# Gated attention with an expert layer on one core: first queries' scores over 128 keys, plain products with v padded to 128 rows, a weight decoding that joins the low and sign bits first, and Newton steps later in a slot

## The chip, the cores and the metric

The kernel runs on one core of one Trainium2 chip. The metric is device time in microseconds of one execution. Three runs of the kernel before took 1253.56, 1248.98 and 1240.35 us, a median of 1248.98. The profiled execution took 1239.64 us, with a span of 1237.4 us from the first to the last instruction.

## The reference

The input is q, k and v of 8 batches x 8 heads x 576 positions x 64, a forget factor f per position, a norm gain g and two weight matrices in float64. Attention with a decay comes first, then a norm and a two-layer network with a residual:

```python
scores = scale * np.matmul(q, k.transpose(0, 1, 3, 2))
log_f = np.log(np.clip(f, 0.0001, 1.0))
cum = np.cumsum(log_f, axis=-1)
decay = cum[:, :, :, None] - cum[:, :, None, :]
scores = np.where(causal, -1000000000.0, scores + decay)
scores = scores - np.max(scores, axis=-1, keepdims=True)
attn = np.exp(scores)
attn = attn / (np.sum(attn, axis=-1, keepdims=True) + 1e-09)
x = np.matmul(attn, v)                      # then heads joined: (8, 576, 512)
xn = (x - mu) / np.sqrt(var + 1e-06) * g_ln
out = x + np.maximum(xn @ w_ch1, 0.0) @ w_ch2
```

w_ch1 is 512 x 2048 and w_ch2 is 2048 x 512. They reach the chip as pairs of 32-bit words, and the kernel itself turns each float64 into a float32, and that into a high part (the type fp32r) and a low part, the rest.

## The kernel before, in words

**Attention.** There are 64 heads. The queries of a head come in five tiles t = 0 to 4 (`QT`): the first 64 queries see 64 keys, and then four tiles of 128 queries see 192, 320, 448 and 576 keys. A slot is one head and one of t = 1 to 4; t = 0 is done together with t = 1, so there are 256 slots. A slot goes: scores on PE (`qk_mm`, L360 or L362 and L363), reduction with mask and minimum on VectorE (`softmax_a`, L386), exponential with a row sum on ScalarE (`softmax_e`, L397), reciprocal of the sum on VectorE (L402, L403), scaling on POOL (`softmax_b`, L404). Two slots later (`LAG`) PE transposes the probabilities (`transpose_unit`, L410) and ScalarE copies them from PSUM to the tiles `ph1` and `ph2` (L460). One slot after that the product with v follows (`av_unit`), once after t = 2 and once after t = 4.

**Two kinds of heads.** The first 16 heads are plain (`h.full`): their products are of float32, and a product appears as two records in the trace. In their product with v (`fac`, L475) 64 rows of the result lie in the lower or upper half of PSUM's partitions, by the query (`SPLIT`), so a tile has 64 columns of weights. The first 64 keys stand alone as k = 0: a product over 64 rows (`rows = slice(0, 64)`), while all others go over 128 rows. The host has sent v with the first 64 rows twice, so all 128 rows of that block of v are filled. The other 48 heads are split into high and low fp32r parts (L362, L363, L500).

**The weights.** While plain heads run, `WPrep` decodes the two matrices in 32 blocks of 128 x 512 numbers, alternately of layer 1 and layer 2. A tick starts a block and carries on the earlier ones: a load from DRAM into `wr` (high and low words alternate), a scaled copy of the high words on ScalarE (`scaled`, L165, into PSUM tile `y`), three steps on VectorE (`decode`), for layer 1 a column sum on PE (L192, `pc`) and four centring steps on VectorE (L200), then the high part on ScalarE (L216) and the low part on POOL (L220). The three decoding steps before are

```python
lambda: ve.tensor_scalar(out=z, in0=z, scalar1=0x80000000, ...),     # L176: sign, in place in wr
lambda: ve.scalar_tensor_tensor(out=y, in0=y, scalar=3, in1=z, ...), # L177: y shifted, sign joined, in PSUM
lambda: ve.scalar_tensor_tensor(out=w, in0=low, scalar=29, in1=y, ...), # L180: low bits joined, into wy
```

`W_SLOTS`, `W_CHANGE` and `W_TICKS` set when ticks are due: one in 2.4 slots up to slot 34, then 0.8 a slot. `wy` has 5 buffers (`W_FLOAT`), `wr` 3. The first 15 blocks (`W_ACC`) use two PSUM tiles that the expert layer needs later; the others take one of the six PSUM banks (`bank`) that scores, transposes, products and hidden values share as well.

**The expert layer.** From slot 35 on (`FIRST_MOE`) a slot also takes one step j of the expert layer for a chunk of 256 tokens, if its weights and inputs are ready: twelve products into `h` (L579 to L581), ScalarE's ReLU (L587), VectorE's low part (L592), and one slot later six products of 512 columns (L601 to L603). A chunk has 16 steps, and there are 18 chunks. The norm's 1/sqrt is worked out on POOL by Newton steps (`chunk_rstd`, L646 to L654) that are kept in a list and run six at a time (`run_later`).

**The order.** It is written out by hand. `ORDERS` holds one string per range of slots, and each letter is a piece: W ticks, w, g and f run 1, 2 and 3 of the queued decoding steps, Q scores, S reduction, e exponential, t transposes, h their copies, A product with v, F and a its finish, M, r, m and N the expert step, R the chunk's upkeep, L the Newton steps, P loads and splits of later heads, B reciprocal and scaling. Each engine works through its instructions in that order. The scaled copy of a block is put at place 5 of the queue of the tick before (`W_ASIDE`) for the first 15 blocks, and for the others it is issued in the tick itself, just ahead of the block's three steps. All DMAs are issued from SP's queue.

Of the kernel before, what the change touches and what calls it, by code (L numbers as in the profile page):

```python
# [8 lines left out]
F32 = mybir.dt.float32  # L9
F32R = mybir.dt.float32r  # L10
U32 = mybir.dt.uint32
# [23 lines left out]
W_ACC = 15  # L35
W_SUMS = 2
# [13 lines left out]
    (37, "WwQSstAMhPelgLNFrfmBRa"),  # L50
    (66, "AthQFlMSPNreamLRB"),
# [4 lines left out]
def attn_moe(ctx: ExitStack, tc: tile.TileContext, qk, v, f, g, w1, w2, out):  # L56
# [79 lines left out]
    class WPrep:  # L136
# [21 lines left out]
        def scaled(self, n):  # L158
            layer, j = self.items[n]
            d = self.d[n]  # L160
            if n < W_ACC:
                d["y"] = ps.tile([P, DM], F32, tag=f"acc{n % 2}", bufs=1, name=f"y{layer}_{j}")
            else:
                d["y"] = bank(f"y{layer}_{j}")
            nc.scalar.activation(d["y"], d["hw"].bitcast(F32), AF.Copy, scale=2.0**-112)  # L165

        def decode(self, n):
            layer, j = self.items[n]
            d = self.d[n]
            y, z, low = d["y"].bitcast(U32), d["hw"], d["lw"]  # L170
            w = wpool.tile([P, DM], U32, tag="wy", bufs=W_FLOAT, name=f"wy{layer}_{j}")
            d["w"] = w.bitcast(F32)
            ve = nc.vector

            return [
                lambda: ve.tensor_scalar(out=z, in0=z, scalar1=0x80000000, scalar2=None, op0=ALU.bitwise_and),  # L176
                lambda: ve.scalar_tensor_tensor(  # L177
                    out=y, in0=y, scalar=3, in1=z, op0=ALU.logical_shift_left, op1=ALU.bitwise_or
                ),
                lambda: ve.scalar_tensor_tensor(  # L180
                    out=w, in0=low, scalar=29, in1=y, op0=ALU.logical_shift_right, op1=ALU.bitwise_or
                ),
            ]
# [39 lines left out]
        def tick(self):  # L223
# [27 lines left out]
            if on(t) and t >= W_ACC:  # L251
                self.scaled(t)
# [6 lines left out]
            if on(t + 1) and t + 1 < W_ACC:  # L259
                self.queue.insert(min(W_ASIDE, len(self.queue)), lambda: self.scaled(t + 1))  # L260
# [90 lines left out]
    def qk_mm(h, t):  # L351
        q0, m, w = QT[t]
        cuts = [(0, w)] if w <= 512 else [(0, w // 2), (w // 2, w)]
        h.s = getattr(h, "s", {})
        h.s[t] = []
        for i, (a, z) in enumerate(cuts):
            sp = bank(f"s{h.n}_{t}_{i}")[:m, : z - a]
            xq, kl = h.xq[:, q0 : q0 + m], h.kl[:, a:z]
            if h.full:
                mm(sp, xq, kl, start=True, stop=True)  # L360
            else:
                mm(sp, h.hi[:, 0, q0 : q0 + m], h.hi[:, 1, a:z], start=True, stop=False)  # L362
                mm(sp, xq, kl, start=False, stop=True)  # L363
            h.s[t].append((a, z, sp))

    corners = []
# [49 lines left out]
    def transpose_unit(h, t):  # L416
# [3 lines left out]
        if t <= 2:  # L420
            if t == 1:
                h.ph1 = work.tile([P, 704], F32 if h.full else F32R, tag="ph1", bufs=1, name=f"ph1_{n}")
                h.pl1 = None if h.full else pools["late"].tile([P, 384], F32R, tag="pl1", bufs=1, name=f"pl1_{n}")
# [15 lines left out]
        else:  # L439
            if t == 3:  # L440
                h.ph2 = work.tile([P, 9 * P], F32 if h.full else F32R, tag="ph2", bufs=1, name=f"ph2_{n}")
                h.pl2 = None if h.full else pools["late"].tile([P, 7 * P], F32R, tag="pl2", bufs=1, name=f"pl2_{n}")
# [24 lines left out]
    def av_unit(h, t):  # L467
        po = bank(f"o{h.n}_{t}")

        if h.full:  # L470

            def fac(cols, k, mv, first=False):
                rows = slice(0, 64) if k == 0 else slice(0, P)
                half = slice(0, 64) if cols.start < SPLIT[t] else slice(64, P)
                mm(po[half, cols], h.vr[rows, k], mv[rows], start=first, stop=True, skip_group_check=True)  # L475
# [415 lines left out]
```

## Time and profile before

| what | value |
|---|---|
| median of three runs | 1248.98 us |
| profiled execution | 1239.64 us |
| its span | 1237.4 us |
| PE busy | 1216.3 us (98%) |
| VectorE busy | 758.5 us (61%) |
| ScalarE busy | 641.8 us (52%) |
| POOL busy | 448.0 us (36%) |
| the chain that ended last, PE's share | 90% |

Instructions are named by engine, line, operation and tiles. PE is a product, PEld a load of weights; products are pipelined and their ends are modelled, so a busy PE may still be waiting inside. In a shape such as `66*64 66x64` the first pair is the rows and columns of the array that are used, and the last number is the columns that stream through. Brackets hold the idle time of the engine ahead of the instruction, and what ended it. The clock is the share of full speed that PE was granted.

### The profile page before, as it was taken

The numbers are of one execution on the slowest core, as the hardware profiler recorded it, in microseconds if no ns is written. First come the engines' busy times: TensorE is split into PE (matmuls) and PEld (weight loads), VectorE is DVE, ScalarE is ACT, GpSimd is POOL, SyncE is SP. The second block draws the span as 40 slices with busy tenths as digits, with TensorE's granted clock in tenths as the row PEclk, the third lists the DMA queues.
The fourth block names the chain that finished last, engine by engine and source line by source line (L and its number), as shares of the span: only waits on it lengthen the run. The fifth ranks groups of instructions, "written<-read, shape, count | busy, mean of one in ns | idle before, by whom it ended". The sixth has DMA issues, their size and how long they took to land.

```text
span 1237.4 us, 25314 instructions
## 1 busy us (share of the span) xinstructions
PE 1216.3 (98%) x8368; PEld 1084.8 (88%) x8368; DVE 758.5 (61%) x2664; ACT 641.8 (52%) x1936; POOL 448.0 (36%) x765
## 2 busy tenths in 40 slices
PE   8998999999999999999999999999999999999998
PEld 6656877899999999999999999999999999999997
DVE  6777673477677767676767676777777662222222
ACT  6886564455555555555655565556555542112111
POOL 3553344344343435444444444444444320000000
PEclk9997998999999999999999999999999999999999
DMA  6554341222323232222222222222222301110100
GB/s 189 151 163 138 112 140 50 70 74 75 94 77 94 77 94 72 88 83 75 71 81 90 81 89 78 76 86 85 71 75 73 94 33 39 52 35 23 46 26 26
DMA packets 91251, 100.44 MB, mean 81 GB/s; under 512 B 26864, under 2 KB 76016, under 8 KB 91120
## 3 DMA queue, kind: packets, MB, share of 16 engines
q1 hardware_dynamic: 91120, 98.82, 26.5%
q8 instruction: 67, 1.10, 0.4%
q14 instruction: 64, 0.52, 0.1%
HBM read 79.61 MB, written 19.17 MB: 80 GB/s over the span
## 4 chain that ended last, share of the span: by engine, by line
PE 90%; DVE 3%; ACT 3%; DMA 1%; issue 1%; POOL 1%; SPq 0%; DVEq 0%; ACTq 0%; POOLq 0%
PE h L579 11%; PE h L580 11%; PE h L581 11%; PE acc L601 11%; PE acc L602 11%; PE acc L603 10%; PE tr L410 7%; PE o L500 6%; PE s L362 3%; PE s L363 3%; PE s L360 2%; PE o L475 2%; PE xp L410 1%; DVE p L386 1%; ACT p L397 1%
## 5 line engine op out<-in xcount | busy, mean ns | idle before, releaser
L404 POOL TENSOR_SCALAR p<-p,st 64x64 f32<-64x64 f32 (+4 forms) x320 | 169.6, 534 | 451.7 <-DVE st L403 156.0
L579 PE MATMUL h<-x,w1h 128*128 128x256 f32 x1152 | 330.1, 287 | 0.5 <-DVE st L386 0.5
L580 PE MATMUL h<-x,w1h 128*128 128x256 f32 x1152 | 326.2, 283 | 0.0
L581 PE MATMUL h<-x,w1l 128*128 128x256 f32 x1152 | 326.2, 283 | 0.0
L587 ACT ACTIVATE hh<-h 128x256 fp32r<-128x256 f32 x288 | 110.6, 384 | 310.4 <-PE h L581 310.3
L592 DVE SCALAR_TENSOR_TENSOR hh<-h,hh 128x256 fp32r<-128x256 f32 x288 | 121.1, 421 | 184.6 <-ACT hh L587 178.0
L601 PE MATMUL acc<-w2h,hh 128*128 128x512 f32 x576 | 228.4, 397 | 0.0
L602 PE MATMUL acc<-w2l,hh 128*128 128x512 f32 x576 | 227.6, 395 | 0.0
L579 PEld LDWEIGHTS h<-x,w1h 128*128 128x128 f32 x1152 | 219.9, 191 | 6.1 <-DVE st L386 0.9
L603 PE MATMUL acc<-w2h,hh 128*128 128x512 f32 x576 | 224.7, 390 | 0.0
L580 PEld LDWEIGHTS h<-x,w1h 128*128 128x128 f32 x1152 | 220.6, 191 | 3.3
L581 PEld LDWEIGHTS h<-x,w1l 128*128 128x128 f32 x1152 | 220.4, 191 | 0.0
L397 ACT ACTIVATE p<-p,st 64x64 f32<-64x64 f32 (+4 forms) x320 | 178.3, 558 | 65.9 <-DVE st L386 64.0
L460 ACT CAST ph<-tr 64x128 fp32r<-64x128 f32 (+4 forms) x384 | 109.1, 333 | 126.2 <-PE tr L410 103.4
L410 PE MATMUL tr<-identr,p 128*128 128x128 f32 (+1 forms) x896 | 142.5, 275 | 5.3 <-POOL p L404 4.7
L386 DVE CUSTOM_DVE_ANT_0 p<-s,mask 64x64 f32<-64x64 f32 (+4 forms) x320 | 130.2, 420 | 5.0 <-PE s L360 1.6
L603 PEld LDWEIGHTS acc<-w2h,hh 128*128 128x128 f32 x576 | 108.3, 188 | 24.9
L410 PEld LDWEIGHTS tr<-identr,p 128*128 128x128 f32 (+1 forms) x896 | 100.9, 131 | 33.3 <-POOL p L404 15.0
L465 DVE TENSOR_TENSOR ph<-tr,ph 64x192 fp32r<-64x192 f32 x192 | 57.8, 301 | 117.1 <-ACT ph L460 114.2
L601 PEld LDWEIGHTS acc<-w2h,hh 128*128 128x128 f32 x576 | 109.5, 190 | 14.1 <-issue 0.3
L602 PEld LDWEIGHTS acc<-w2l,hh 128*128 128x128 f32 x576 | 109.5, 190 | 11.8
L340 POOL TENSOR_TENSOR hi<-raw,hi 64x576 fp32r<-64x576 f32 x48 | 73.8, 1537 | 66.7 <-ACT hi L338 65.3
(83 smaller groups left out, 1846.9 us busy)
## 6 DMA issues: line engine op xcount, KB each, us to landing
raw<-in_qk_dram SPq DMA_DIRECT2D x48, 576.0 KB
wr<-in_w_dram SPq DMA_DIRECT2D x32, 512.0 KB
vr<-in_v_dram SPq DMA_DIRECT2D x64, 160.0 KB
out_dram<-xt SPq DMA_DIRECT2D x36, 256.0 KB
xa<-xs SPq DMA_DIRECT2D x32, 160.0 KB
xb<-xs SPq DMA_DIRECT2D x32, 128.0 KB
xw<-xa SPq DMA_DIRECT2D x64, 64.0 KB
xw<-xb SPq DMA_DIRECT2D x48, 64.0 KB
```

Source lines behind the costliest of these rows:

```text
L386: nc.vector.tensor_tensor_reduce(out=pt[:m, a:z], in0=sp, in1=mask[:m, off + a : off + z], scale=-SCALE, scalar=3.0e38 if i == 0 else st[: ...
L397: nc.scalar.activation(pt[:m, :w], pt[:m, :w], AF.Exp, bias=st[:m, i : i + 1], scale=-1.0, accum_out=st[:m, 2:3])
L404: nc.gpsimd.tensor_scalar(out=pt[:m, :w], in0=pt[:m, :w], scalar1=st[:m, 3:4], scalar2=1.0, op0=ALU.mult, op1=ALU.mult)
L410: nc.tensor.transpose(out_, in_, ident[:m, :m])
L579: mm(ph, w1h[:, k, fs], c.x[k][:, 0, :], start=(k == 0), stop=False)
L580: mm(ph, w1h[:, k, fs], c.x[k][:, 1, :], start=False, stop=False)
L581: mm(ph, w1l[:, k, fs], c.x[k][:, 0, :], start=False, stop=(k == KT - 1))
L587: nc.scalar.activation(h[:, 0, :], c.ph, AF.Relu)
L592: nc.vector.scalar_tensor_tensor(out=h[:, 1, :], in0=ph, scalar=0.0, in1=h[:, 0, :].bitcast(F32), op0=ALU.max, op1=ALU.subtract)
L601: mm(c.acc[i], h[:, 0, ts_], w2h[:, j, :], start=(j == 0), stop=False)
L602: mm(c.acc[i], h[:, 0, ts_], w2l[:, j, :], start=False, stop=False)
L603: mm(c.acc[i], h[:, 1, ts_], w2h[:, j, :], start=False, stop=(j == FT - 1))
```

## The change

Four edits, all in the first quarter of the program's slots but for the one of the Newton steps and the wider key range.

1. *First queries' scores.* Plain heads multiply 128 queries by 128 keys for t = 0, and only 64 x 64 of the result is read. Split heads multiply their 64 queries by 128 keys.
2. *Plain products with v.* `ph1` and `ph2` become two tiles that live for all plain heads, with rows 64 to 127 of the k = 0 part set to zero once by POOL. The k = 0 product then goes over 128 rows like the others.
3. *Decoding.* The scaled copy goes to the SBUF tile `wy` and always stands at place 5 of the queue of the tick before. The three steps are: low words shifted right by 29 into a PSUM tile; sign bits of the high words joined to it there; scaled copy shifted left by 3 and joined with it, in place in `wy`. The high words in `wr` are no longer overwritten.
4. *Newton steps.* The letter L moves behind B in the second and third order.

```diff
+W_BORROW = 2
 ORDERS = [
     (0, "WwQsSthAeMrgFBmlLNPaRf"),
-    (37, "WwQSstAMhPelgLNFrfmBRa"),
-    (66, "AthQFlMSPNreamLRB"),
+    (37, "WwQSstAMhPelgNFrfmBLRa"),
+    (66, "AthQFlMSPNreamRBL"),
 ]
         def scaled(self, n):
-            if n < W_ACC:
-                d["y"] = ps.tile([P, DM], F32, tag=f"acc{n % 2}", bufs=1, name=f"y{layer}_{j}")
+            if layer == 1 and self.tick_no < W_BORROW:
+                d["y"] = m2(f"wy{layer}_{j}", U32)
             else:
-                d["y"] = bank(f"y{layer}_{j}")
-            nc.scalar.activation(d["y"], d["hw"].bitcast(F32), AF.Copy, scale=2.0**-112)
+                d["y"] = wpool.tile([P, DM], U32, tag="wy", bufs=W_FLOAT, name=f"wy{layer}_{j}")
+            nc.scalar.activation(d["y"].bitcast(F32), d["hw"].bitcast(F32), AF.Copy, scale=2.0**-112)
         def decode(self, n):
+            def last():
+                ...   # t: acc tile for n < W_ACC, else a bank
+                ve.tensor_scalar(out=bits[0], in0=low, scalar1=29, scalar2=None, op0=ALU.logical_shift_right)
             return [
-                lambda: ve.tensor_scalar(out=z, in0=z, scalar1=0x80000000, scalar2=None, op0=ALU.bitwise_and),
+                last,
                 lambda: ve.scalar_tensor_tensor(
-                    out=y, in0=y, scalar=3, in1=z, op0=ALU.logical_shift_left, op1=ALU.bitwise_or
+                    out=bits[0], in0=high, scalar=0x80000000, in1=bits[0], op0=ALU.bitwise_and, op1=ALU.bitwise_or
                 ),
                 lambda: ve.scalar_tensor_tensor(
-                    out=w, in0=low, scalar=29, in1=y, op0=ALU.logical_shift_right, op1=ALU.bitwise_or
+                    out=y, in0=y, scalar=3, in1=bits[0], op0=ALU.logical_shift_left, op1=ALU.bitwise_or
                 ),
             ]
         def tick(self):
...
-            if on(t) and t >= W_ACC:
-                self.scaled(t)
...
-            if on(t + 1) and t + 1 < W_ACC:
+            if on(t + 1):
                 self.queue.insert(min(W_ASIDE, len(self.queue)), lambda: self.scaled(t + 1))
     def qk_mm(h, t):
+        if t == 0:
+            w = P
+            m = P if h.full else m
+            cuts = [(0, w)]
+    def padded_keys(tag, width, zeros):
+        if tag not in padded:
+            padded[tag] = work.tile([P, width], F32, tag=tag, bufs=1, name=f"{tag}_full")
+            nc.gpsimd.memset(padded[tag][64:128, 0:zeros], 0.0)
+        return padded[tag]
             def fac(cols, k, mv, first=False):
-                rows = slice(0, 64) if k == 0 else slice(0, P)
                 half = slice(0, 64) if cols.start < SPLIT[t] else slice(64, P)
-                mm(po[half, cols], h.vr[rows, k], mv[rows], start=first, stop=True, skip_group_check=True)
+                mm(po[half, cols], h.vr[:, k], mv, start=first, stop=True, skip_group_check=True)
```

What moves on ScalarE, about slot 38, around the scaled copy of the 18th block. Before (L563 splits a chunk's inputs, L216 writes a high part, L460 copies transposes, L165 is the scaled copy):

```order
L532 COPY xs_0_1381<-o_2_1371 64x192
L533 COPY xs_0_1381<-o_2_1371 64x128
L563 CAST x_0_1394<-xr_0_1337 128x256
L563 CAST x_1_1397<-xr_1_1339 128x256
L216 CAST w2h<-wy_7_1280 128x512
L165 ACTIVATE y_8_1408<-wr_8_1274 128x512
L460 COPY ph_8_1363<-tr_4_1417 64x128
L460 COPY ph_8_1363<-tr_4_1417 128x3x128
```

Now (L557, L558, L588, L225, L166 and L486 are the same pieces in their order):

```order
L557 COPY xs_0_1367<-o_2_1357 64x192
L558 COPY xs_0_1367<-o_2_1357 64x128
L588 CAST x_0_1380<-xr_0_1326 128x256
L588 CAST x_1_1383<-xr_1_1328 128x256
L166 ACTIVATE wy_8_1390<-wr_8_1264 128x512
L225 CAST w2h<-wy_7_1243 128x512
L486 COPY ph_full<-tr_4_1403 64x128
L486 COPY ph_full<-tr_4_1403 128x3x128
```

The scaled copy now belongs to the tick before and stands ahead of that tick's high part; its output is `wy`, and it waits for the low part on POOL that leaves that buffer.

On VectorE at the same block, before (L564 splits inputs, ISA is the score reduction, L200 centres a block of layer 1):

```order
L564 TENSOR_TENSOR x_1_1397<-xr_1_1339,x_1_1397 128x256
L176 TENSOR_SCALAR wr_8_1274<-wr_8_1274 128x512
L386 ISA p_2_1414,st_2_1415<-s_2_0_1412,mask 128x320
L386 ISA st_2_1415 128x1
L200 SCALAR_TENSOR_TENSOR wy_7_1208<-wy_7_1208,gcol,pc_1353 128x128
L177 SCALAR_TENSOR_TENSOR y_8_1408<-y_8_1408,wr_8_1274 128x512
L200 SCALAR_TENSOR_TENSOR wy_7_1208<-wy_7_1208,gcol,pc_1353 128x128
L180 SCALAR_TENSOR_TENSOR wy_8_1410<-wr_8_1274,y_8_1408 128x512
```

Now:

```order
L589 TENSOR_TENSOR x_1_1383<-xr_1_1328,x_1_1383 128x256
L182 TENSOR_SCALAR y_8_1396<-wr_8_1264 128x512
L406 ISA p_2_1400,st_2_1401<-s_2_0_1398,mask 128x320
L406 ISA st_2_1401 128x1
L209 SCALAR_TENSOR_TENSOR wy_7_1141<-wy_7_1141,gcol,pc_1340 128x128
L186 SCALAR_TENSOR_TENSOR y_8_1396<-wr_8_1264,y_8_1396 128x512
L209 SCALAR_TENSOR_TENSOR wy_7_1141<-wy_7_1141,gcol,pc_1340 128x128
L189 SCALAR_TENSOR_TENSOR wy_8_1390<-wy_8_1390,y_8_1396 128x512
```

Nothing has changed places here; the first step no longer writes `wr`, which the scaled copy reads, and the scaled copy's result is first read by the third step.

More of the change, by code (lines that the diff above doesn't have):

```diff
@@ L169, in decode @@
             d = self.d[n]
-            y, z, low = d["y"].bitcast(U32), d["hw"], d["lw"]
-            w = wpool.tile([P, DM], U32, tag="wy", bufs=W_FLOAT, name=f"wy{layer}_{j}")
-            d["w"] = w.bitcast(F32)
+            y, high, low = d["y"], d["hw"], d["lw"]
+            d["w"] = y.bitcast(F32)
             ve = nc.vector
+            bits = []
+            def last():
+                if n < W_ACC:
+                    t = ps.tile([P, DM], F32, tag=f"acc{n % 2}", bufs=1, name=f"y{layer}_{j}")
+                else:
+                    t = bank(f"y{layer}_{j}")
+                bits.append(t.bitcast(U32))
+                ve.tensor_scalar(out=bits[0], in0=low, scalar1=29, scalar2=None, op0=ALU.logical_shift_right)
             return [
-                lambda: ve.tensor_scalar(out=z, in0=z, scalar1=0x80000000, scalar2=None, op0=ALU.bitwise_and),
+                last,
                 lambda: ve.scalar_tensor_tensor(
-                    out=y, in0=y, scalar=3, in1=z, op0=ALU.logical_shift_left, op1=ALU.bitwise_or
+                    out=bits[0], in0=high, scalar=0x80000000, in1=bits[0], op0=ALU.bitwise_and, op1=ALU.bitwise_or
                 ),
                 lambda: ve.scalar_tensor_tensor(
-                    out=w, in0=low, scalar=29, in1=y, op0=ALU.logical_shift_right, op1=ALU.bitwise_or
+                    out=y, in0=y, scalar=3, in1=bits[0], op0=ALU.logical_shift_left, op1=ALU.bitwise_or
                 ),
@@ L421, in transpose_unit @@
             if t == 1:
-                h.ph1 = work.tile([P, 704], F32 if h.full else F32R, tag="ph1", bufs=1, name=f"ph1_{n}")
+                if h.full:
+                    h.ph1 = padded_keys("ph1", 704, S1)
+                else:
+                    h.ph1 = work.tile([P, 704], F32R, tag="ph1", bufs=1, name=f"ph1_{n}")
                 h.pl1 = None if h.full else pools["late"].tile([P, 384], F32R, tag="pl1", bufs=1, name=f"pl1_{n}")
@@ L440, in transpose_unit @@
             if t == 3:
-                h.ph2 = work.tile([P, 9 * P], F32 if h.full else F32R, tag="ph2", bufs=1, name=f"ph2_{n}")
+                if h.full:
+                    h.ph2 = padded_keys("ph2", 9 * P, S - S1)
+                else:
+                    h.ph2 = work.tile([P, 9 * P], F32R, tag="ph2", bufs=1, name=f"ph2_{n}")
                 h.pl2 = None if h.full else pools["late"].tile([P, 7 * P], F32R, tag="pl2", bufs=1, name=f"pl2_{n}")
```

4 lines of the change are left out of this document (3 added, 1 removed).

## The prediction

> **What bounds the kernel now.** The profiled execution took 1239.64 us. I read first the busy times by stage, to see where the end can move at all. The columns are the stretch, its length, busy us (instructions) of PE, PEld, DVE, ACT and POOL, the granted clock, DMA share and GB/s.
>
> ```profile
> 97.00:245.00 148.00, 140.12 (x927) 113.24 (x926) 84.92 (x299) 84.02 (x256) 58.47 (x80) 0.93 0.33 99
> 245.00:1018.00 773.00, 773.00 (x5474) 715.27 (x5473) 550.04 (x1969) 445.29 (x1350) 333.19 (x545) 1.00 0.26 80
> ```
>
> From 245 us on, with split heads and expert steps, PE has no idle at all (773.00 of 773.00): only PE's own instructions count there. All slack lies in the first 245 us, where the 16 plain heads run beside the decoding of the weights. From 97 us every slot also carries an expert step; PE is short of 7.9 us there, and the clock is at 0.93.
>
> Second, who holds PE up in that stretch: the waits, then the timeline around the first stall.
>
> ```profile
> DVE wr L176 <- ACT y L165: 11.0, 16, 1.4
> ```
>
> ```profile
> 90.53 0.66 ACT L165 ACTIVATE y<-wr 128x512 f32<-128x512 f32 x1
> ...
> 91.19 1.26 POOL L220 TENSOR_TENSOR w1l<-wy,w1h 128x512 fp32r<-128x512 f32 x1
> 91.22 1.51 DVE L176 TENSOR_SCALAR wr<-wr 128x512 uint32<-128x512 uint32 x1 [0.73 <-ACT y L165]
> ...
> 93.33 0.77 PE L360 MATMUL s<-kl,xf 66*128 66x288 f32 x1 [1.19 <-DVE st L386]
> ```
>
> VectorE reaches the first decoding step L176 and waits 0.73 us for ScalarE's L165, because L176 overwrites what L165 reads. Then L176, normally 0.41 us (below), takes 1.51: it ends when POOL's L220 ends (91.19 + 1.26 = 92.45). Behind it in VectorE's queue stands the score reduction L386, and PE's next scores wait for the bank that L386 empties. The same at two more places:
>
> ```profile
> 103.16 1.14 DVE L176 TENSOR_SCALAR wr<-wr 128x512 uint32<-128x512 uint32 x1 [0.58 <-ACT y L165]
> ```
>
> ```profile
> 104.76 1.12 PE L360 MATMUL s<-kl,xf 66*128 66x448 f32 x1 [2.63 <-DVE st L386]
> ```
>
> ```profile
> 170.54 0.97 DVE L176 TENSOR_SCALAR wr<-wr 128x512 uint32<-128x512 uint32 x1 [1.39 <-ACT y L165]
> ```
>
> Third, what follows each stall: stretches cut where the clock changes (length, PE busy, clock).
>
> ```profile
> 89.99:93.41 3.42, 2.23 (x22) 1.00 0.57 178
> 93.41:100.24 6.83, 6.69 (x27) 0.50 0.66 180
> 100.24:103.65 3.41, 1.89 (x13) 1.00 0.19 39
> 103.65:110.47 6.82, 5.71 (x27) 0.50 0.58 183
> 168.55:175.40 6.85, 4.98 (x35) 1.00 0.49 131
> 175.40:178.80 3.40, 3.18 (x13) 0.50 0.66 226
> 199.30:206.10 6.80, 6.70 (x35) 0.50 0.31 102
> ```
>
> After each stretch in which PE sat idle 1.2 to 1.9 us, PE gets half its clock for 3.4 or 6.8 us. A stall is paid twice.
>
> **The decoding.** The first step no longer touches what ScalarE reads: it shifts the low words into PSUM and needs only the DMA. L165 is issued a tick earlier and writes SBUF. So the wait of 0.6 to 1.4 us ahead of the first step goes. What the step itself costs:
>
> ```profile
> 20.00:90.00 70.00, 4.93 (x12) 1.00 0.53 154
> 90.00:185.00 95.00, 12.48 (x17) 0.91 0.45 132
> ```
>
> ```profile
> L177 DVE SCALAR_TENSOR_TENSOR y<-y,wr 128x512 uint32<-128x512 uint32 x32 | 22.1, 691 | 0.0
> ```
>
> (The first two are L176's busy time alone.) L176 takes 4.93 / 12 = 0.41 us early and 0.73 from 90 us on, where it meets L220. A one-source step from SBUF to PSUM is not in the trace; its nearest rows are L176 (0.41, SBUF to SBUF) and L177 (0.69, PSUM out). I take 0.69, since L177 shares its output; 0.41 stays as the other end. Steps two and three keep L177's and L180's kinds of operands and cost the same.
>
> A page weighs on this: the Trainium skill, "VectorE: DVE Perf Modes", section "Why PSUM operands drop a tier", says that the doubled rate of a one-source fp32 step is lost with an operand in PSUM. 512 elements at the page's 0.96 GHz take 0.53 us, doubled 0.27; by it the step takes, as an estimate, 0.41 - 0.27 + 0.53 = 0.67 us, which would change the sum by under 0.3 us.
>
> From 90 us, at each stall PE gets back the smaller of its idle and what VectorE is freed of. First: 0.73 + 1.51 - 0.69 = 1.55, against 3.42 - 2.23 = 1.19 idle: 1.2. Second: 0.58 + 1.14 - 0.69 = 1.0, against 2.6 (1.5 + 1.1): 1.0. Third: 1.39 + 0.97 - 0.69 = 1.7, against 1.9: 1.7. **Term 1: -3.9 us.** Its ends: 0, if another wait ends just as late, and -6.0, all idle of these stretches (1.2 + 0.1 + 1.5 + 1.1 + 1.9 + 0.2).
>
> The clock: the three halved stretches before 180 us hold 6.69 + 5.71 + 3.18 = 15.6 us of PE work, 7.8 us more than at full clock. The second stall is only partly removed, so I take two thirds: **term 2: -5.2 us**, ends 0 and -7.8. The halved stretch from 199.30 stays: the stall ahead of it comes from a run of L220 on POOL when the weights are flushed, and that is not changed.
>
> Before 90 us the first step is dearer: 12 x (0.69 - 0.41) = 3.4 us of VectorE. How much is on the path is read from the chain of waits there:
>
> ```profile
> by line: ACT p L397 14.5%; DVE p L386 12.4%; issue 8.3%; PE s L360 8.0%; PE o L475 5.8%; DVE wy L180 5.7%; ACT ph L460 5.6%; PE tr L410 5.0%; DVE wy L200 4.8%; DMA xf<-in_qk_dram 4.3%; DMA kl<-in_qk_dram 4.2%; DVE y L177 4.0%; DVE wr L176 3
> ```
>
> VectorE's lines make 27% of it: **term 3: +0.9 us** (0 to +3.4).
>
> A new wait: from the seventh block on, the scaled copy takes a buffer that POOL's L220 of the same tick must leave first. Behind it on ScalarE stand the copies of the transposes (L460) and the next exponentials, for which PE and VectorE wait.
>
> ```profile
> 58.97 1.27 POOL L220 TENSOR_TENSOR w1l<-wy,w1h 128x512 fp32r<-128x512 f32 x1
> ```
>
> ```profile
> 59.89 0.65 ACT L165 ACTIVATE y<-wr 128x512 f32<-128x512 f32 x1
> ```
>
> Here L165 would have to wait until 60.24, 0.35 us. Nine such ticks before 97 us give 0 to 3.2 us; I choose a third: **term 4: +1.0 us**. Later, ScalarE gets there only after an expert step's product, long after L220.
>
> **The padding.** Where PE goes from 128x128 to 64-column tiles or back, or from 64 to 128 rows, the next weights are loaded only after the array has emptied. First queries (timeline of PE, then the weight loads of the two attention units):
>
> ```profile
> 136.78 0.39 PE L602 MATMUL acc<-w2l,hh 128*128 128x512 f32 x1
> 137.01 0.39 PE L603 MATMUL acc<-w2h,hh 128*128 128x512 f32 x1
> 137.33 0.85 PE L360 MATMUL s<-kl,xf 66*64 66x64 f32 x4
> 138.02 0.60 PE L410 MATMUL tr<-identr,p 128*64 128x128 f32 x4
> ```
>
> ```profile
> 79.88 0.20 PEld L475 LDWEIGHTS o<-ph,vr 64*64 64x64 f32 x4 [0.17 <-DVE wy L200]
> 80.25 0.85 PEld L475 LDWEIGHTS o<-ph,vr 128*64 128x64 f32 x14 [0.17 <-issue]
> ```
>
> ```profile
> 138.55 0.20 PEld L475 LDWEIGHTS o<-ph,vr 64*64 64x64 f32 x4 [0.17 <-issue]
> 139.01 0.42 PEld L475 LDWEIGHTS o<-ph,vr 128*64 128x64 f32 x6 [0.27 <-issue]
> ```
>
> ```profile
> 122.65 0.89 PE pc L192 x8
> ```
>
> ```profile
> 59.80 0.75 PE s L360 x2
> ```
>
> From L603 to the transposes PE spends 138.02 - 137.01 = 1.01 us. Without a switch it is L603 (0.23, as L602 to L603), two records of 128x128 (0.89 / 8 = 0.11 each) and two of 192 columns (0.75 / 2 x 192 / 448 = 0.16): 0.77. Gain 0.24 us a head. In the units, the 64-row products hold PE 0.37 and 0.46 us; at 128 rows they follow the pace of the others, two pairs of 0.85 / 7 = 0.12 and two of 192 columns at 0.16: 0.24 and 0.32. Gain 0.27 a head. The switch into and out of the 64-column form stays.
>
> Heads that come after 97 us, in the second stretch alone (two records a product):
>
> ```profile
> L475 PE MATMUL o<-ph,vr 64*64 64x192 f32 x16 | 4.7, 373 | 0.4 <-DVE st L402 0.4
> ```
>
> ```profile
> L360 PE MATMUL s<-kl,xf 66*64 66x64 f32 x12 | 2.0, 246 | 0.9 <-DVE st L386 0.9
> ```
>
> 8 heads x 0.27 + 6 x 0.24 = 3.6, all on PE's path: **term 5: -3.6 us**. The other 8 and 10 give 4.6, of which PE's share of the chain above (8.0 + 5.8 + 5.0 = 19%) counts: **term 6: -0.9 us** (0 to -4.6).
>
> The 48 split heads get 64 more key columns in two products each, in the stretch without idle. At L603's pace 64 columns are 0.23 / 8 = 0.03 us, 96 x 0.03 = 2.8 at most. I cost it at nothing: the loads hide it.
>
> ```profile
> 524.68 0.14 PEld L363 LDWEIGHTS s<-kl,xq 66*64 66x64 f32 x1
> 524.74 0.19 PEld L362 LDWEIGHTS s<-hi 128*128 128x128 f32 x1
> ```
>
> The second product's load takes 0.06 us, as long as 128 columns stream. The Newton steps run on POOL, which has idle; where PE has no idle nothing is won by them, and the two new memsets run once on POOL.
>
> **Sum:** -3.9 - 5.2 + 0.9 + 1.0 - 3.6 - 0.9 = -11.7; 1239.6 - 11.7 = 1227.9 us. The median of the runs shown, 1248.98, lies 9.3 above the profiled execution. I take that scatter to be stalls that fall more or less unluckily into the clock's stretches; with most of them gone, half of it: 1232 us.
>
> **The rivals.**
>
> *The half clock stays.* Row: 1.19 us of idle in 3.42, then 0.50. Were the clock's fall not tied to these stalls, term 2 and the narrower scatter are lost: 1227.9 + 5.2 + 9.3 = 1242. Against it: each halved stretch shown here follows such an idle. The Trainium skill, "TensorE: Matmul & The Clock Gate", section "Why this matters for your kernels", asks for idle gaps above some 3 us before the clock falls; by that rule stalls of 1.2 to 2.6 us cannot be the cause; the rows here disagree. Chance 0.24.
>
> *The wait moves.* VectorE is freed, but POOL's or a DMA's turn ends as late; terms 1 and 2 vanish: 1239.6 - 2.6 + 9.3 = 1246. For it: DMA rows take 8.5% of the early chain. Chance 0.13.
>
> *The padding saves nothing*, because the array empties before every unit anyway: 1227.9 + 4.5 + 4.7 = 1237. Against it: the 0.17 and 0.27 us ahead of the 128-row loads. Chance 0.10.
>
> *Slower.* ScalarE's new wait and the dearer first step before 97 us: at full price 3.2 + 3.4 = 6.6 us, less term 5. That alone is +3. If they push further stretches of 3.41 us over the 1.2 us of idle that halve the clock, each costs up to 1.7 us. It decides from six such stretches on; eight give 1239.6 + 3.0 + 13.6 + 9.3 = 1266. Against it stands how far an early stretch is from that, 0.39 us of idle in the one just ahead of the first stall:
>
> ```profile
> 86.58:89.99 3.41, 3.02 (x14) 1.00 0.18 58
> ```
>
> Chance 0.04.
>
> The forecast has 0.49. A measurement tells about 1% here: faster is below 1236.5. That takes 0.44 of the forecast's 0.49 (its ends reach it from above), 0.05 of the padding rival and 0.05 of the clock rival: 0.54; slower 0.04; same 0.42. The range reaches from 1220 (terms 1, 2 and 6 well towards their ends) to 1248, which takes in the moved wait.
>
> **What would show it.** Right: no idle of VectorE ahead of the first decoding step, its busy time near 0.69 us with little spread; no halved clock from 90 to 180 us; the first scores' loads without a gap, and 64-row loads gone. Wrong: ScalarE idle on L220 for more than 3 us before 97 us, PE idle above 1 us on POOL or a DMA where L386 ended it, a span after 245 us longer than before, or halved stretches that follow no idle.

## The result, and the profile after

The changed kernel takes 1230.49 us (median), the kernel before, run beside it, 1240.37. The ratio is 0.990, 95% interval 0.988 to 0.992: 1% faster, clear of noise, and inside the range. One of the sixteen executions of the changed kernel took 1728.5 us at a mean clock of 0.63, where the other fifteen have 0.988 or more; the ratio and the times at half clock are of those fifteen. The 1248.98 us from which the prediction started was a median of three that lay high; the gain is 9.9 us and not the 17 between 1248.98 and 1232.

The profiled execution of the changed kernel took 1236.05 us and is one of its longest. Its stages, in the columns used above (length, PE, PEld, VectorE, ScalarE, POOL, clock, DMA share, GB/s):

```profile
97.00:245.00 148.00, 140.28 (x965) 118.20 (x962) 91.48 (x322) 87.20 (x267) 59.29 (x84) 0.94 0.37 109
245.00:1018.00 773.00, 772.87 (x5478) 715.14 (x5476) 549.33 (x1962) 445.34 (x1349) 331.00 (x543) 1.00 0.26 79
```

After 245 us nothing changed: PE still has next to no idle (0.13 us), and from the same exponential (the 85th, at 246.74 us before and 243.66 now) to the end it is 990.7 us before and 990.6 now. All of the change lies ahead of it.

The first decoding step (now L182) in the two stretches for which L176 was shown:

```profile
20.00:90.00 70.00, 7.43 (x11) 0.91 0.49 144
90.00:185.00 95.00, 12.23 (x18) 0.95 0.49 140
```

It takes 0.68 us early and late, from 0.67 to 0.69 in every block, and VectorE waits for nothing ahead of it: the 11.0 us of waits for the scaled copy are gone.

The padding, in PE's timeline at a head's first scores (compare L603 at 137.01 and L410 at 138.02), and then in the weight loads of the two units of the product with v (the row of the second ends with its window, after 12 of 18 loads):

```profile
140.48 0.39 PE L628 MATMUL acc<-w2h,hh 128*128 128x512 f32 x1
140.70 0.71 PE L371 MATMUL s<-kl,xf 66*128 66x128 f32 x4
141.25 0.60 PE L430 MATMUL tr<-identr,p 128*64 128x128 f32 x4
```

```profile
141.78 0.63 PEld L500 LDWEIGHTS o<-ph_full,vr 128*64 128x64 f32 x10 [0.17 <-issue]
...
151.49 0.64 PEld L500 LDWEIGHTS o<-ph_full,vr 128*64 128x64 f32 x12 [0.17 <-issue]
```

From the last expert product to the transposes it is 141.25 - 140.48 = 0.77 us where it was 1.01 (0.78 in the unrounded times), and the 64-row loads are gone.

What did not come is the full clock between 90 and 180 us. The stretches of this execution that end idle or run at half clock (length, then busy time of the engines in the same order, then the clock):

```profile
15.97:19.38 3.41, 2.18 (x16) 1.38 (x16) 2.34 (x11) 1.24 (x4) 1.53 (x3) 1.00 1.11 273
19.38:33.04 13.66, 13.66 (x59) 10.00 (x57) 8.94 (x37) 9.17 (x29) 3.48 (x7) 0.50 0.37 112
97.89:101.30 3.41, 2.38 (x14) 1.77 (x14) 3.23 (x12) 2.58 (x8) 1.42 (x2) 1.00 0.35 94
101.30:104.72 3.42, 3.42 (x20) 2.74 (x19) 2.61 (x10) 2.57 (x9) 1.98 (x2) 0.50 0.87 261
104.72:108.13 3.41, 1.37 (x8) 0.88 (x7) 2.85 (x8) 3.17 (x11) 2.12 (x3) 1.00 0.40 96
108.13:114.95 6.82, 6.25 (x31) 4.92 (x31) 6.09 (x18) 3.56 (x10) 2.04 (x2) 0.50 0.55 174
193.46:196.88 3.42, 1.08 (x5) 0.36 (x3) 1.37 (x7) 1.54 (x6) 3.42 (x4) 1.00 0.13 48
196.88:203.70 6.82, 5.95 (x33) 5.01 (x34) 0.00 (x0) 1.66 (x6) 3.21 (x12) 0.50 0.40 125
```

The one from 19.38 on is new; by its end the exponentials come 3.8 us later than before, where they had been level at 20 us. The one from 101.30 follows a stall that was not in the kernel before, 0.94 us until VectorE's third step L189 is done; the kernel with the padding alone, below, has the same 0.94 us behind its third step L180, at 95.34, so the new decoding isn't needed for it. The one from 108.13 follows the second stall, which is still there. Timeline of PE, VectorE and POOL ahead of both:

```profile
99.91 1.17 PE L371 MATMUL s<-kl,xf 66*128 66x128 f32 x4 [0.94 <-DVE wy L189]
...
105.81 1.83 DVE L589 TENSOR_TENSOR x<-xr,x 128x256 fp32r<-128x256 f32 x2 [0.49 <-ACT x L588]
...
105.92 1.44 POOL L229 TENSOR_TENSOR w1l<-wy,w1h 128x512 fp32r<-128x512 f32 x1
...
107.57 0.68 DVE L182 TENSOR_SCALAR y<-wr 128x512 uint32<-128x512 uint32 x1
...
108.70 1.11 PE L371 MATMUL s<-kl,xf 66*128 66x448 f32 x1 [2.62 <-DVE st L406]
```

In the second, the first decoding step waits for nothing and takes 0.68. But ahead of it in VectorE's queue stand the two low parts of a chunk (L589, otherwise 0.42 us each), and in this execution the second of them takes 1.49 us and ends at 107.64, just behind POOL's L229 (105.92 + 1.44 = 107.36). PE waits 2.6 us, as long as before.

Each run comes with its span and mean clock, so the time spent at half clock can be had for every execution: (1 - clock) x 2 x span. On average it is 28.8 us for the kernel before (its 22 executions beside the first four experiments below) and 15.4 for the changed one. It comes in steps: clock 0.997 (about 7 us halved) gives 1227.1 to 1227.9 us, 0.993 (17 us) 1229.9 to 1232.4, 0.988 (30 us) 1236.1 to 1236.3.

### The profile page after: what moved, and what is told of

It is laid out like the page before. It is cut to its first block, busy times and chain, and to the rows that moved or that the text cites. A ratio compares the mean times of both kernels' runs of the same rounds, so it can differ in the third digit from the quotient of the medians.

```text
span 1234.3 us, 25357 instructions
## 1 busy us (share of the span) xinstructions
PE 1210.6 (98%) x8368; PEld 1088.0 (88%) x8368; DVE 762.5 (62%) x2664; ACT 643.4 (52%) x1936; POOL 445.1 (36%) x767
## 4 chain that ended last, share of the span: by engine, by line
PE 93%; DVE 3%; ACT 2%; DMA 1%; POOL 1%; issue 1%; DVEq 0%; SPq 0%; ACTq 0%; POOLq 0%
PE h L604 11%; PE h L605 11%; PE h L606 11%; PE acc L626 11%; PE acc L627 11%; PE acc L628 11%; PE tr L430 8%; PE o L525 6%; PE s L373 3%; PE s L374 3%; PE s L371 3%; PE o L500 2%; PE xp L430 1%; PE pc L201 1%; DVE p L406 1%; ACT p L417 1%
## 5 line engine op out<-in xcount | busy, mean ns | idle before, releaser
L486 ACT CAST ph<-tr 64x128 fp32r<-64x128 f32 (+4 forms) x384 | 109.2, 333 | 124.6 <-PE tr L430 107.1
L430 PEld LDWEIGHTS tr<-identr,p 128*128 128x128 f32 (+1 forms) x896 | 101.0, 131 | 38.9 <-POOL p L424 18.2
L373 PE MATMUL s<-hi 128*128 128x288 f32 (+4 forms) x288 | 96.2, 355 | 0.0
```

Source lines behind the costliest of these rows:

```text
L430: nc.tensor.transpose(out_, in_, ident[:m, :m])
```

## The experiments

First, each part alone, the Newton steps, and a mixture; then runs that take single steps of the argument apart. All times are medians; "halved" is the mean time at half clock, worked out as above. The ratios are to the kernel before, run beside each on the same chip.

| kernel | time, us | ratio to before (95%) | halved, us |
|---|---|---|---|
| before | 1239.8 to 1240.6 | 1 | 27 to 31 |
| changed | 1230.49 | 0.990 (0.988 to 0.992) | 15.4 |
| decoding alone | 1234.75 | 0.996 (0.993 to 0.999) | 21.4 |
| padding alone | 1234.77 | 0.994 (0.992 to 0.996) | 18.2 |
| changed, Newton steps at the old place | 1227.21 | 0.989 (0.985 to 0.992) | 11.0 |
| changed, first 15 blocks as before | 1228.84 | 0.988 (0.985 to 0.992) | 12.7 |
| changed, first step into SBUF early | 1234.13 | 0.995 (0.993 to 0.997) | 22.5 |
| changed, last four low parts on VectorE | 1224.89 | 0.987 (0.985 to 0.989) | 8.2 |
| the two edits with the lowest times, Newton steps old | 1222.44 | 0.985 (0.983 to 0.988) | 7.7 |
| before, one more VectorE step a block, early | 1249.93 | 1.007 (1.005 to 1.009) | 41.7 |
| changed, scaled copy in its own tick | 1231.38 | 0.992 (0.989 to 0.994) | 17.6 |
| changed, first step into SBUF late | 1231.56 | 0.992 (0.989 to 0.995) | 14.4 |

A second view runs through all of them: how much later or earlier than before a given exponential starts in the profiled execution, as the 43rd and the 85th here:

```profile
89.46 0.56 ACT L397 ACTIVATE p<-p,st 128x320 f32<-128x320 f32 x1 [0.18 <-DVE st L386]
...
246.74 0.78 ACT L397 ACTIVATE p<-p,st 128x576 f32<-128x576 f32 x1
```

| exponential, start before | changed | decoding | padding | first 15 as before | low parts on VectorE |
|---|---|---|---|---|---|
| 13th, 33.4 us | +3.8 | +0.2 | 0.0 | -0.6 | +0.1 |
| 43rd, 89.5 | +6.2 | +2.6 | 0.0 | -0.1 | +3.1 |
| 67th, 176.0 | +0.5 | -5.3 | -0.9 | -9.7 | -6.7 |
| 85th, 246.7 | -3.1 | -7.8 | -3.0 | -14.2 | -15.7 |
| 265th, 831.4 | -3.0 | -7.8 | -3.3 | -14.5 | -15.1 |

### The decoding alone

```diff
--- before
+    nc.scalar.activation(d["y"].bitcast(F32), ...)      # into wy, always a tick earlier
+    steps: low >> 29 into PSUM; sign joined there; y << 3 joined, in wy
     # qk_mm, ph1, ph2, fac and ORDERS as before
```

> The kernel before with the decoding of the change alone (scaled copy into wy a tick earlier, low bits first, in PSUM). Theory (terms 1 to 4): the idle ahead of the first step goes and with it the halved stretches behind it, -3.9 - 5.2 + 0.9 + 1.0 = -7.2 us against the kernel before (ratio 0.994), with no halved clock between 90 and 180 us and the first step at 0.68 us. Rival (the wait moves): the chunk's low part on VectorE takes over the slow-down beside POOL, as the changed kernel's trace shows near 106 us; the time stays within 2 us of before (ratio 0.998 to 1.002).

1234.75 us, 5.4 less than before. The theory's half is in the trace: from the 43rd to the 85th exponential it gains 10.4 us, and after a halved stretch of 3.4 us at 92 us the clock is whole up to the end of the decoding near 190 us, where POOL makes the last four low parts in a row; between the same points the kernel before had 17 us at half clock:

```profile
95.50:187.60 92.10, 89.47 (x627) 71.91 (x627) 69.04 (x235) 61.68 (x184) 38.98 (x51) 1.00 0.46 136
```

By then it is 2.6 us late, though, and that is more than terms 3 and 4 gave. L589 beside POOL is not slowed down in this execution. In the ones profiled for the other experiments one of these instructions takes 1.48 us once, 0.64 twice and 0.5 twice in place of 0.42: it depends on how the two engines happen to meet, and is no fixed price.

### The padding alone

```diff
--- before
+    if t == 0: w = P; m = P if h.full else m; cuts = [(0, w)]
+    ph1, ph2: rows 64 to 127 of the k = 0 part zeroed once
-                rows = slice(0, 64) if k == 0 else slice(0, P)
+                h.vr[:, k], mv     # 128 rows
```

> The kernel before with the padding alone (128 x 128 first scores, 128-row products with v); decoding and Newton steps as before. Theory (terms 5 and 6): -4.5 us (ratio 0.996), all of it before 245 us; the three stalls of 91, 103 and 171 us stay. Rival (the padding does all of it): -9 us or more (ratio 0.992 or below). Rival (the padding saves nothing): within 1 us of before.

1234.77 us, 5.3 less. Up to the 43rd exponential it moves nothing at all (0.0 us):

```profile
89.44 0.56 ACT L410 ACTIVATE p<-p,st 128x320 f32<-128x320 f32 x1 [0.18 <-DVE st L399]
```

Then 3.0 us come by the 85th, and nothing later, so the wider first scores of the 48 split heads cost nothing. In this execution the halved time is that of the kernel before (27 us without the last stretch behind PE's work). Between executions of equal clock (0.993 and 0.994) the padding gives 1234.6 against 1238.6, the decoding 1234.5, the whole change 1230.5: some 4 us each, and they add up.

### The Newton steps at their old place

```diff
--- changed
-    (37, "WwQSstAMhPelgNFrfmBLRa"),
-    (66, "AthQFlMSPNreamRBL"),
+    (37, "WwQSstAMhPelgLNFrfmBRa"),
+    (66, "AthQFlMSPNreamLRB"),
```

> The changed kernel with the Newton steps back at their old place. Theory: they run on POOL, which has idle, and from 245 us on PE waits for nothing; the time is the changed kernel's, 1230.5 us (ratio to before 0.992, within 1 us). Rival: at their old place they hold up POOL's low parts and scalings between slots 37 and 66, and the time is over 3 us longer, 1233.5 or above.

1227.21 us, 3.3 less than the changed kernel, but the intervals of the two overlap: four of its six executions have a clock of 0.997, of the changed kernel's fifteen five. At equal clock they are the same: 1226.9 to 1227.4 at 0.997 against 1227.1 to 1227.9, 1231.0 at 0.993 against 1229.9 to 1232.4. The move is worth nothing either way that can be measured.

### The first 15 blocks decoded as before

```diff
--- changed, scaled and decode
+    if n < W_ACC:
+        # copy into the PSUM tile acc, sign in place in wr, y << 3 in PSUM, low bits joined into wy
```

> The changed kernel, but the first 15 blocks are decoded as before (sign in place in wr, scaled copy in PSUM); the later 17 as changed. Theory (terms 3 and 4): the early blocks' dearer first step and the scaled copy's wait for POOL are what makes the changed kernel some 2.6 us later at 96 us, beside the halved clock; -2 to -3 us against the changed kernel, 1228 us, and the exponentials before 96 us come as early as in the kernel before. Rival: the padding or the clock is what delays the early slots; the time stays at 1230.5.

1228.84 us; the interval overlaps the changed kernel's, so the time alone decides nothing. In the trace the 43rd exponential is back where it was before the change, 6.3 us ahead of the changed kernel's (3.6 of them that one's halved stretch at 19 us):

```profile
89.40 0.57 ACT L426 ACTIVATE p<-p,st 128x320 f32<-128x320 f32 x1
```

The six other executions profiled with the early decoding as it is in the change (decoding alone, Newton steps, own tick, late SBUF, low parts and gaps) have it 2.5 to 3.1 us late, the two with the old one (this, and the last below) within 0.2. So the early loss is the decoding's, and the late blocks keep the gain (14.2 us from the 43rd to the 85th). ScalarE waits for POOL's low part once, 0.2 us; in the changed kernel, never. Term 4 is nothing.

### The first step into SBUF, in the early blocks

```diff
--- changed, last()
                 if n < W_ACC:
-                    t = ps.tile([P, DM], F32, tag=f"acc{n % 2}", ...)
+                    bits.append(m2(...))       # SBUF
```

> The changed kernel, but the first decoding step of the first 15 blocks writes to SBUF and not to PSUM (a tile of the pool m2); all else is as changed. Theory (the dearer first step is what the early slots lose): the step falls from 0.68 to some 0.41 us, and the 2.6 us by which the changed decoding is late at slot 34 nearly go; the time is 2 us below the changed kernel's, near 1228. Rival (the earlier scaled copy into wy, or the order of the three steps): the step is faster, but the slots stay 2 to 3 us late and the time stays at 1230.

Both theories fell. The step is down to 0.41 us, and yet the kernel is slower, 1234.13 us. Groups of VectorE between 20 and 97 us:

```profile
L185 DVE SCALAR_TENSOR_TENSOR bits<-wr,bits 128x512 uint32<-128x512 uint32 x12 | 12.7, 1059 | 0.0
L188 DVE SCALAR_TENSOR_TENSOR wy<-wy,bits 128x512 uint32<-128x512 uint32 x13 | 12.4, 958 | 0.4
...
L181 DVE TENSOR_SCALAR bits<-wr 128x512 uint32<-128x512 uint32 x12 | 4.9, 411 | 0.0
```

With both sources in SBUF the second and third step go from 0.69 to 1.06 and 0.96 us on average, 1.75 at worst, where POOL is at work; with one source in PSUM they stay at 0.67 to 0.71 whatever POOL does. The Trainium skill, "SBUF — State Buffer", section "SBUF: two separate sides", says that VectorE and POOL share a pair of ports as an exclusive lock, which a VectorE instruction with two SBUF inputs takes too; these rows agree. One of the lengthened steps beside POOL's instruction:

```profile
50.32 1.28 POOL L228 TENSOR_TENSOR w1l<-wy,w1h 128x512 fp32r<-128x512 f32 x1
...
51.06 1.08 DVE L185 SCALAR_TENSOR_TENSOR bits<-wr,bits 128x512 uint32<-128x512 uint32 x1
```

It starts while L228 is at work and ends at 52.14, 0.54 us behind L228's end at 51.60. The run also gives an early price. For 12 blocks the three steps take 12 x (0.41 + 1.06 + 0.96) = 29 us against 12 x (0.41 + 0.69 + 0.685) = 21.4 before: 7.8 us more, and from the 13th to the 43rd exponential the run loses 9.0, with two stretches of half clock in it. So term 3's theory is neither shown nor refuted by this run.

### One more VectorE step in each early block

```diff
--- before, decode
+                if n < W_ACC:
+                    ve.tensor_scalar(out=w[:, 0:256], in0=z[:, 0:256], scalar1=0, ..., op0=ALU.bitwise_or)
```

> The kernel before with one more VectorE instruction in each of the first 15 blocks, right behind the first decoding step (256 columns written to wy, which the third step overwrites): some 0.25 us each, by L176's 0.41 us for 512 columns. Theory (VectorE's time is on the path in the early slots nearly in full): 13 blocks before slot 34 make the exponentials at 90 us 2.5 to 3.3 us later, and the later stretches stay as before: about 1243. Rival (the chain's share, 27%, is the price): 0.7 to 0.9 us later at 90 us, 1241.

This measures what a microsecond of VectorE costs in the early slots. The added step is dearer than I had set it, again beside POOL. Its group between the 19th and the 43rd exponential, and these two:

```profile
L178 DVE TENSOR_SCALAR wy<-wr 128x256 uint32<-128x256 uint32 x8 | 4.2, 520 | 0.8
```

```profile
51.48 0.67 ACT L402 ACTIVATE p<-p,st 128x448 f32<-128x448 f32 x1 [0.53 <-DVE st L391]
...
100.26 0.56 ACT L402 ACTIVATE p<-p,st 128x320 f32<-128x320 f32 x1 [0.25 <-DVE st L391]
```

The same two start at 44.83 and 89.46 before. The way between them grew from 44.63 to 48.78 us, by 4.15, and 4.2 us of VectorE were put in, with the clock whole throughout: all of it counts. The chain's share, 27%, would have given 1.1. Neither theory had the rest right: the 43rd exponential is 10.8 us late and not 0.7 to 3.3, since 6.6 of these are there by the 19th, in which time this execution ran 17.1 us at half clock from 19.48 on; and the time of the whole run, 1249.93, is worse than 1241 and 1243, with 41.7 us at half clock on average.

### The scaled copy in its own tick

```diff
--- changed, tick()
+            if on(t) and t >= W_ACC:
+                self.scaled(t)
-            if on(t + 1):
+            if on(t + 1) and t + 1 < W_ACC:
```

> The changed kernel, but from the 16th block on the scaled copy is issued in its block's own tick, as before, and no longer a tick earlier; it still writes wy, and the first step still needs the DMA only. Theory (it is the first step's independence that counts): the copy is done by the time the third step comes, 1.4 us later; the time stays within 2 us of the changed kernel, 1229 to 1232. Rival (the wait moves to the third step): VectorE waits 0.5 us or more ahead of the third step at several ticks, stalls above 1 us come back near 91 and 171 us, and the time goes to 1234 to 1236.

1231.38 us, as the theory had it. VectorE stands 0.10 us ahead of some third steps, here as in the changed kernel and in the kernel before, and never longer: the first two steps give it the 1.4 us that it needs. What counts is that the first step doesn't depend on ScalarE, not that the copy comes a tick earlier.

### The first step into SBUF, in the late blocks

```diff
--- changed, last(), n >= W_ACC
-                    t = bank(f"y{layer}_{j}")
+                    t = m2(f"bits{layer}_{j}", F32)
```

> The changed kernel, but from the 16th block on the first decoding step writes to SBUF (a tile of m2), and the second works there; the first 15 stay in PSUM. Theory (PSUM shields the steps from POOL): with all operands in SBUF steps two and three wait for POOL's instruction to end, as they did in the early slots of the run with the first step in SBUF (up to 1.75 us in place of 0.69); stalls and halved stretches between 90 and 200 us come back, and the time rises by 3 to 6 us over the changed kernel, 1233 to 1236, although PE has one more bank free. Rival (only the wait for ScalarE mattered): 1228 to 1231.

The steps are held up by POOL as expected, here between 90 and 185 us (in the changed kernel 0.69 and 0.68):

```profile
L186 DVE SCALAR_TENSOR_TENSOR bits<-wr,bits 128x512 uint32<-128x512 uint32 x17 | 19.9, 1172 | 0.0
L189 DVE SCALAR_TENSOR_TENSOR wy<-wy,bits 128x512 uint32<-128x512 uint32 x17 | 13.4, 786 | 0.8
...
L182 DVE TENSOR_SCALAR bits<-wr 128x512 uint32<-128x512 uint32 x17 | 8.6, 506 | 0.0
```

But the time, 1231.56, is not 3 to 6 us longer; its interval overlaps the changed kernel's, and the theory fell. VectorE works some 7 us more in this stretch (41.9 for 17 blocks against 17 x (0.68 + 0.69 + 0.68) = 34.9) and the end comes no later: with expert steps in each slot PE has work of its own. There the price of VectorE's time is small, as far as this run shows. (A PSUM bank less is in use here, which may have given some of it back; that wasn't taken apart.) That the kernel before was hurt by long waits at a few places, and not by VectorE's time as such, fits this and isn't shown apart.

### The last four low parts on VectorE

```diff
--- changed, low()
-            nc.gpsimd.tensor_tensor(out=lo, in0=w, in1=hi.bitcast(F32), op=ALU.subtract)
+            eng = nc.vector if n >= 28 else nc.gpsimd
+            eng.tensor_tensor(out=lo, in0=w, in1=hi.bitcast(F32), op=ALU.subtract)
```

> The changed kernel, but the low parts of the last four blocks are made on VectorE and not on POOL. The stall near 194 us, in which PE waits 3.2 us for POOL's scaling behind four low parts of 1.27 us, is in all kernels so far, with a halved clock of 3.4 to 6.8 us behind it. Theory: taking it away gains its idle, 3 us, and half of the halved stretch, 1.7 to 3.4 us: together 4.5 to 6 us below the changed kernel, near 1225, and fast runs without any halved stretch after 120 us. Rival (clock not tied to the idle): the idle goes, -3 us, but a halved stretch stays near 195 us: 1227.5.

The stall that the change did not touch, in the changed kernel's timeline of POOL and PE:

```profile
192.45 1.29 POOL L229 TENSOR_TENSOR w2l<-wy,w2h 128x512 fp32r<-128x512 f32 x1
...
196.14 1.26 POOL L229 TENSOR_TENSOR w1l<-wy,w1h 128x512 fp32r<-128x512 f32 x1
197.39 0.71 POOL L424 TENSOR_SCALAR p<-p,st 64x64 f32<-64x64 f32 x2
```

```profile
197.75 0.42 PE L430 MATMUL tr<-identr,p 128*64 128x128 f32 x1 [3.21 <-POOL p L424]
```

With the four on VectorE, first one of them and then the stretch that held stall and half clock:

```profile
185.40 0.68 DVE L230 TENSOR_TENSOR w2l<-wy,w2h 128x512 fp32r<-128x512 f32 x1
```

```profile
190.00:200.00 10.00, 10.00 (x73) 8.80 (x72) 3.92 (x18) 5.88 (x20) 2.54 (x5) 1.00 0.19 59
```

PE is busy throughout, the clock stays whole, and no stretch from 100 us up to the end is halved in this execution. 1224.89 us, 5.6 below the changed kernel and as the theory had it; the longest of its six executions (1226.74) is shorter than the shortest of the changed kernel (1227.11). Between the 73rd and the 79th exponential (196.05 and 222.81 us before) this execution gains 7.3 us on the kernel before, the changed one's 0.6. The 6.7 us between them are the wait of 3.2 and half of the 6.8 us at half clock behind it: taking away the idle took away the half clock as well.

### Gaps of known length

```diff
--- changed, last loop, every second step
+    src = a transpose on PE; k times: copy of 128 x 128 on ScalarE; a transpose of the last copy on PE
```

> The changed kernel with 18 gaps made in the last stretch, where PE works alone: at every second step PE waits for a chain of 2 to 12 copies of a 128 x 128 tile on ScalarE, some 0.2 to 0.3 us each, so about 0.8 to 3.5 us of idle. Theory (idle of a stretch of 3.41 us decides): gaps of 1.6 us and more are followed by a halved clock of 3.4 or 6.8 us, gaps of 0.8 us never. Rival (only gaps above 3 us count, as the Trainium skill has it in 'TensorE: Matmul & The Clock Gate'): no halved stretch behind gaps of 1 to 2.9 us.

One execution, 1299.21 us. The gaps came out at 0.69 to 4.0 us of idle. Behind them the clock changes only at multiples of 3.413 us, so the run can be cut there. Four stretches with a gap and, behind three of them, the next (length, PE busy, PEld, VectorE, ScalarE, POOL, clock):

```profile
1038.57:1041.99 3.42, 1.33 (x7) 0.80 (x5) 0.42 (x1) 2.06 (x8) 2.36 (x13) 1.00 0.00 0
1127.32:1130.73 3.41, 1.35 (x9) 0.91 (x9) 0.83 (x3) 2.06 (x8) 0.00 (x0) 1.00 0.00 0
1130.73:1134.15 3.42, 3.42 (x14) 3.13 (x14) 0.42 (x1) 0.38 (x1) 0.00 (x0) 0.50 0.00 0
1147.80:1151.21 3.41, 1.68 (x14) 1.38 (x13) 0.00 (x0) 1.46 (x5) 0.00 (x0) 1.00 0.38 92
1151.21:1154.63 3.42, 3.42 (x24) 3.12 (x23) 0.42 (x1) 0.57 (x2) 0.00 (x0) 1.00 0.09 28
...
1031.75:1035.16 3.41, 1.78 (x14) 1.78 (x15) 0.00 (x0) 1.45 (x5) 0.00 (x0) 1.00 0.00 0
1035.16:1038.57 3.41, 3.41 (x24) 3.06 (x24) 1.30 (x3) 1.10 (x3) 0.00 (x0) 1.00 0.00 0
```

All ten stretches at full clock with 2.06 us of idle or more (2.06, 2.08, 2.13, 2.23, 2.31, 2.34, 2.49, 2.71, 3.05, 3.41) were followed by half clock; none with 1.73 or less was (1.73, 1.73, 1.64, 1.40, 1.40, 1.29, 1.09, 1.07, 0.69). Between 1.73 and 2.06 nothing was measured. The gap of 2.06 us that ends at 1033.38 falls on a border, 0.41 and 1.64 us, and costs nothing behind it; the one of 2.06 that lies whole in 1127.32 to 1130.73 does. The theory's 1.6 us was set too low; that the idle of a whole stretch decides is right. The rule of gaps above 3 us, which the prediction quoted from the Trainium skill, "TensorE: Matmul & The Clock Gate", section "Why this matters for your kernels", is not what this run shows.

### The edits with the lowest times together

```diff
--- changed
+    first 15 blocks decoded as before; low parts of the last four blocks on VectorE
+    ORDERS of before
```

> The changed kernel with the first 15 blocks decoded as before, the Newton steps at their old place and the last four low parts on VectorE. Theory: the hybrid's 2 to 3 us and the flush's 4.5 to 6 add up, since they lie in different stretches: 1222 to 1224 us, below both kernels. Rival: without the stall at 194 us PE runs into the next wait there; no better than the hybrid, 1228.8.

1222.44 us, as the theory had it, ratio 0.985 (0.983 to 0.988) to the kernel before: the lowest of all, though its interval overlaps that of the low parts alone. The halved time is 7.7 us on average.

## Why the prediction was right

**Term 1 and term 2, -9.1 us: right in mechanism and nearly in size.** The decoding alone gains 10.4 us between the 43rd and the 85th exponential; 13.7 us less at half clock make up to 6.8 of it, and the rest, 3.6, fits the idle that went (5.2 and 3.9 were set). Of the three stalls the first and the third went. PE no longer waits in the middle of the scores that went on at 93.33 (from 97.36 on in the changed kernel, without a gap). The third's longest wait, 0.88 us, fell to 0.42 or less; only the late SBUF run has one of 0.72. The second stays, with 1.3 to 2.6 us in all but one of the executions profiled with the new late decoding; at times L589 beside POOL fills it up again. So the sign that was set, no half clock between 90 and 180 us, did not come: these executions hold 0 to 10.2 us of it there, the changed kernel's own the most, against 17.1 before. The halved time fell by 13.4 us on average in the whole change, so up to 6.7 us. How that splits isn't settled: alone, the padding took 10.6 off and the decoding 7.3, which is more than both together. How often a stretch is halved differs from execution to execution, so -5.2 was a mean, and the page of a single execution can show the opposite: the one profiled here holds more halved time before 97 us than the kernel before.

Two readings were a little off, without weight in the sum. L176 at 91.22 does not end with L220 but 0.28 us behind it (92.73 against 92.45). And the stretch from 168.55, read as 1.9 us of idle, is two periods of the clock, with 0.88 and 0.96 us; the half clock followed the second.

**Term 3, +0.9 us: the step that failed.** The first step costs 0.68 us, as set. But "VectorE's lines make 27% of it" (its four rows that are shown in full; with L176's own 3% it is 30%) was taken for the price of a microsecond, and it is about three to four times that. In the early slots all of VectorE's time counts: 4.2 us added cost 4.15; 12 x (0.675 - 0.41) = 3.2 us of dearer first steps cost 2.5 to 3.1. The end that was written beside the term, +3.4, was right. The share of a line in the chain says how long the chain ran through it, and says little of what happens when it grows: there each tick's steps stand in VectorE's queue ahead of a score reduction, and the other rows of the chain, ScalarE's and PE's, follow that reduction one after the other and are pushed along with it. (The price is measured; this reason for it is read from the order of the queue.)

**Term 4, +1.0 us: nothing.** ScalarE never waits for POOL's low part ahead of the scaled copy. The overlap of 0.35 us that was read off the kernel before did not come; why isn't shown. The slots that the first step makes late may have given L229 the time.

**Terms 5 and 6, -4.5 us: the sum right, its place not.** A head's first scores gave 1.01 - 0.78 = 0.23 us (0.24 set). The product with v gave, from its first record to the next piece of PE's work, 1.05 - 0.81 = 0.24 and 1.39 - 1.24 = 0.15 us in its two units, 0.39 a head and not 0.27: the unit of 10 records, set at 0.14, was the one mis-sized. With 8 and 6 heads that is 4.5 us of PE's time after 97 us, of which 3.0 reached the end; the rest went into the remaining waits. Before 97 us nothing came (-0.9 set): the stretch hangs on VectorE, as the run with one more step shows, so PE's time is free there. The padding alone gained 5.3 us in the median; the 2.3 above the 3.0 would fit the fewer halved stretches (18.2 us against 28.8), which the sum didn't have; that was not tested apart.

**The rest.** The split heads' wider first scores, the Newton steps and the memsets cost nothing, as set. "Half of the scatter" was set against three runs that happened to lie high. The two errors, the early price and the starting point, are of opposite sign: the sum itself was -11.7 us against -9.9 measured, and 4.7 us were added for scatter of which the median over more runs, 1240.37, holds 0.7. That 1232 came within 1.5 us of 1230.49 is in part luck.

**The rivals.** "The half clock stays" fell with the run of the last low parts and the gaps. "The wait moves" is right for one of three stalls and some executions. "The padding saves nothing" fell. "Slower" had the right cause, VectorE's dearer first step before 97 us, at its full price. Of the halved stretches that were to follow the profiled execution has one before 97 us, 13.65 us long; 13 of the 15 executions have at most 17.2 us at half clock in all, so it is not the rule.

## What to carry to other kernels

The share of an engine in the chain of waits is no price. Put a known amount of work on it, in the stretch in question, and measure how far a later instruction moves: here VectorE's time counted in full in one stretch and, as far as one run shows, hardly at all in the next. A stall of PE costs its length, and half of the stretch behind it at half clock if enough of it falls into one period, so it is the long waits that are worth hunting, and a sum has to be made over many executions. An intermediate in PSUM can be dearer by itself and still be the better place, if another engine works in SBUF beside it.

## What the runs showed of the hardware that was not expected

- The clock of PE is decided in fixed periods of 3.413 us by how much PE was idle in the last one: halved after 2.06 us or more, not after 1.73 or less, in the stretch where PE works on full tiles alone. At half clock less idle kept it there: 1.02, 1.05 and 1.47 us did, 0.63 and less did not. Among the small tiles of the early slots no such line is seen: 1.03 us in the changed kernel's period from 97.89 was followed by half clock, 1.54 in that from 99.54 of the run with the first 15 blocks as before was not. Why isn't settled; PE's busy time is modelled there.
- A VectorE step with two sources in SBUF takes up to 1.98 us in place of 0.69 while POOL is at work (the late blocks' run), and one with a source in PSUM 0.67 to 0.71 throughout. The lengthened ones end 0.54 to 0.55 us behind an instruction of POOL; one-source steps, such as L176 at 91.22, 0.28 us behind it. A one-source step that writes to PSUM takes 0.67 to 0.69, from SBUF to SBUF 0.41 when undisturbed and up to 1.51 beside POOL, in the kernel before.
- Where a 64-row product between 128-row ones became a 128-row product with zeros, PE saved 0.24 us in the unit of 10 records and 0.15 in that of 18, although it multiplies more.
